# A tuned three-layer kernel: narrowing of the last layer's weights split in two parts, with a four-buffer target and a later cast

## The chip, the cores and the metric

The kernel runs on one core of a Trainium2 chip. The metric is the device time of one execution in microseconds. The kernel is timed in several runs; one more execution is profiled, and its trace is what the rows below come from. The engines are TensorE (PE, and PEld for its weight loads), VectorE (DVE), ScalarE (ACT), GpSimd (POOL) and SyncE (SP, which issues the transfers). Each takes its instructions strictly in the order of its own queue.

## The reference

Three layers follow each other. An attention with a running state gives 3072 tokens of 384 numbers. A mixture of 8 experts takes each token through one of them (384 to 1024 to 384, with a relu). The last layer is a gated unit whose weights come in 64-bit numbers:

```python
def _moe2_ref(x, w_gate, w_val, w_out):
    gate = 1.0 / (1.0 + np.exp(-(x @ w_gate)))    # w_gate, w_val: 384 x 1536
    val = x @ w_val
    return (gate * val @ w_out).astype(np.float32) # w_out: 1536 x 384
```

## The kernel before

All products run as three passes of a faster matmul type: each operand is split into a high part `h` (a cast on ScalarE) and a low part `l` (the operand minus its high part, on GpSimd or VectorE), and h x h, h x l, l x h are summed.

**The expert stage** (class `Experts`, about 350 to 615 us) works through 36 quarters: nine jobs (token windows) of four. A quarter holds two *places* (`f`), and a place is: nine matmuls `h` (L1151), a relu on ScalarE to `hh` (L1154), its low part `hl` on VectorE (L1155), and then the nine matmuls of the place before into `y` (L1114), of which three need `hl`. The expert weights `w1r` and `w2r` are loaded by SP and split with a cast `w1h`/`w2h` on ScalarE (L1087) and a subtraction `w1l`/`w2l` (L1092), most of them on GpSimd, some on VectorE. Rows of tokens `XR` are loaded from the table `disp`, scaled, and turned into `xh`/`xl`. The instructions that `Queue` issues (line L87) keep the written order; the others are ordered by the framework's scheduler, which takes what its own model of time finds ready. So the program's text sets an order of priority, and buffers and dependences decide what can be taken ahead.

**The last layer's weights** `w_gate` and `w_val` are brought in beside the experts, in 24 blocks of 384 x 128, by `hook`, which is called once in each place; from the 9th quarter on it deals with one block per quarter. Each block is

- loaded by SP as pairs of 32-bit words (`load_wide`, L987) into a tile of the ring XG, which has four buffers;
- narrowed from 64-bit to 32-bit numbers on VectorE by five operations (`narrow`, L998 to L1002): the first two take sign, exponent and upper bits from the high word into the result, the third and fourth make the rest from the low word, in the raw tile, and the fifth adds it. The result goes to the tile `xt`, of which there is one buffer;
- split by `split_hi_lo`: a cast to `wgh` or `wvh` on ScalarE (L974) and a subtraction to `wgl` or `wvl` on GpSimd (L975).

The last layer itself (L1465 on, from 615 us) narrows the 12 blocks of `w_out` with the same `narrow`, into the same `xt`, while its first token block runs.

Of the kernel before, what the change touches and what calls it, by code (L numbers as in the profile page):

```python
# [7 lines left out]
F32 = mybir.dt.float32  # L8
# [3 lines left out]
U32 = mybir.dt.uint32  # L12
AF = mybir.ActivationFunctionType
ALU = mybir.AluOpType
# [15 lines left out]
ROW = 386  # L30
# [941 lines left out]
def split_hi_lo(nc, hi, lo, src, eng, act=None):  # L972

    (act or nc.scalar).copy(out=hi, in_=src)  # L974
    eng.tensor_tensor(out=lo, in0=src, in1=hi, op=ALU.subtract)  # L975


def load_wide(queue, r, src, shape):

    wide = src.dtype != F32  # L980
    r = r[:, 0 : shape[0] * shape[1] * (2 if wide else 1)]
    if not wide:
        r = r.rearrange("p (a b) -> p a b", a=shape[0])
        queue.dma_start(out=r, in_=src)
        return r
    r = r.bitcast(U32)
    queue.dma_start(out=r.rearrange("p (a b) -> p a b", a=shape[0]), in_=src.bitcast(U32))  # L987
    return r.rearrange("p (a b t) -> p a b t", a=shape[0], t=2)


def narrow(nc, t, r):

    if r.dtype == F32:
        return r
    V = nc.vector
    u = t.bitcast(U32)
    lo, hi = r[..., 0], r[..., 1]
    V.tensor_scalar(out=u, in0=hi, scalar1=3, scalar2=0x3FFFFFFF, op0=ALU.logical_shift_left, op1=ALU.bitwise_and)  # L998
    V.scalar_tensor_tensor(out=u, in0=hi, scalar=0xC0000000, in1=u, op0=ALU.bitwise_and, op1=ALU.bitwise_or)
    V.tensor_scalar(out=hi, in0=u, scalar1=0xFF800000, scalar2=None, op0=ALU.bitwise_and)  # L1000
    V.scalar_tensor_tensor(out=lo.bitcast(F32), in0=lo, scalar=2.0**-52, in1=hi.bitcast(F32), op0=ALU.mult, op1=ALU.mult)
    V.tensor_tensor(out=t, in0=lo.bitcast(F32), in1=t, op=ALU.add)  # L1002
    return t


class Job:
# [161 lines left out]
def kernel_body(tc, a, out):  # L1168
    nc = tc.nc
    V, A, G, T, SP = nc.vector, nc.scalar, nc.gpsimd, nc.tensor, nc.sync  # L1170
    with ExitStack() as ctx:
# [10 lines left out]
        if True:  # L1182
# [13 lines left out]
            gs = ctx.enter_context(tc.tile_pool(name="gt_s", bufs=1, side="left"))  # L1196
# [42 lines left out]
            gv = [[yp.tile([128, 3, DF2], F32R, name=n + p) for p in "hl"] for n in ("wg", "wv")]  # L1239
# [40 lines left out]
            def gv_src(i):  # L1280
                b, w = divmod(i, 2)
                return w, slice(128 * b, 128 * b + 128), a[("m2g", "m2v")[w]].rearrange("(c p) f -> p c f", p=128)[:, :, 128 * b : 128 * b + 128]

            wide = {}
# [4 lines left out]
            queued, head = [], []  # L1289

            def first_high():

                for c in range(3):
                    A.copy(out=head[c], in_=y2T[:, c, 0:512])

            def hook(q, f):
                i = 2 * q + f
                if i == 0:
                    E.high(2)
                    E.low(2, 0, E.G)  # L1300
                    tail(1)
                elif i == 1:
                    tail(2)
                    tail(3)
                    E.low(2, 1, E.V)
                elif i == 2:
                    E.high(3)
                    E.low(3, 0, E.V)
                    E.low(3, 1, E.V)
                    E.n_split = 4  # L1310
                elif i == 3:
                    order()
                    E.rows(1)
                    E.load(6)
                if i == QX:
                    E.x_scale(1, (E.V, E.A))
                if i == QT:
                    for c in range(3):
                        E.x_turn(1, c)
                if i in (10, 12):  # L1320
                    E.split(E.n_split + 1)
                if i == 14:
                    queued.append(E.SP)
                    nc_ = tc.nc
                    E.use((nc_.vector, nc_.scalar, nc_.gpsimd, nc_.tensor, nc_.sync))
                if i == 10:
                    E.rows(2)
                if i == QS:
                    E.x_scale(2, (E.V,))
                if i == 13:  # L1330
                    for c in range(3):
                        E.x_turn(2, c)
                if i == SG:
                    A.activation(out=key[:, 0:1], in_=cst[0:1, 0:1], func=AF.Sigmoid)
                if i == YS:
                    head.extend(gs.tile([128, 2, ROW], F32, tag="XG", name="XG", bufs=4).rearrange("p a b -> p (a b)")[:, 0:512].bitcast(F32R) for _ in range(3))
                    first_high()
                if f == 0 or q < 8:
                    return
                q -= 8  # L1340
                if q < 24:
                    r = gs.tile([128, 2, ROW], F32, tag="XG", name="XG", bufs=4).rearrange("p a b -> p (a b)")
                    wide[q] = load_wide(queued[0] if q < 4 else SP, r, gv_src(q)[2], [3, 128])
                if 1 <= q < 25:
                    w, cols, _ = gv_src(q - 1)
                    f = narrow(nc, gs.tile([128, 3, 128], F32, tag="xt", name="xt", bufs=1), wide.pop(q - 1))
                    split_hi_lo(nc, *[t[:, :, cols] for t in gv[w]], f, G)

            with tc.tile_pool(name="ex_p", bufs=1, reuse_waits="tile", space=PSUM) as pp:
                E.run(y2T, pp, gp, hook, True)  # L1350
# [4 lines left out]
            with tc.If(placed < NTOK):  # L1355
                with tc.tile_pool(name="ov", bufs=1) as ov:
                    q = ov.tile([1, 2, 64 + NE * NW_], F32, name="ov_q")
# [47 lines left out]
            with ExitStack() as m2:  # L1405
# [8 lines left out]
                def wo_load(f):  # L1414
                    r = wide[:, 768 * (f % 2) : 768 * (f % 2) + 768]
                    r = load_wide(SP, r, a["m2o"][128 * f : 128 * f + 128].rearrange("p (o d) -> p o d", o=3), [3, 128])
                    r = narrow(nc, gs.tile([128, 3, 128], F32, tag="xt", name="xt", bufs=1), r)
                    split_hi_lo(nc, *[t[:, f].rearrange("p (o d) -> p o d", o=3) for t in wo], r, G)
# [13 lines left out]
                wide = sp.tile([128, 3, 512], F32R, tag="yh", name="yh", bufs=2).bitcast(F32).rearrange("p c t -> p (c t)")  # L1432
# [21 lines left out]
                for tb in range(6):  # L1454
                    Yn = None
                    ops_ = [pp.tile([128, 512], F32, tag=f"o{m}", name=f"o{m}") for m in range(4)]
                    for f in range(12):
# [17 lines left out]
                        if len(pend) == (4 if tb == 5 and f > 8 else 1):  # L1475
                            p = pend.pop(0)
# [75 lines left out]
```

## Time and profile before

| | before |
|---|---|
| median of 3 runs (all) | 1078.68 us (1072.25 to 1078.94) |
| the profiled execution: time, span | 1077.86 us, 1076.2 us |
| TensorE busy | 1016.2 us (94%) |
| VectorE busy | 547.4 us (51%) |
| ScalarE busy | 397.2 us (37%) |
| GpSimd busy | 313.5 us (29%) |

A matmul's end is modelled, so a busy TensorE is not one at its peak; where it is shown idle it did wait. "Held" below means that an operation took longer than its usual time. Times of a stretch are counted from the span's start.

### The profile page before, as it was taken

Reading aid. Unit: us, or ns where it says so; the run is one execution under the profiler, and the core shown is the slowest. Engines: PE = TensorE matmul, PEld = TensorE weight load, DVE = VectorE, ACT = ScalarE, POOL = GpSimd, SP = SyncE. Lnnn points to the kernel's source line nnn. Section 1 sums busy time; section 2 is a strip of 40 time slices with the busy share of each in tenths; the row PEclk is TensorE's granted clock in tenths of the full one; section 3 lists DMA queues with packets and bytes.
Section 4 is the critical chain, followed back from the end, with each engine's and each line's share of the span. In section 5 each row is a group of like instructions: output and inputs, shape, how many; then the busy total and the mean of one; then the engine's idle time right before and its main releaser. Section 6 shows DMA issues by size and latency. Waiting matters only on the chain. (4 is left out here: it accounts for less than half of the span.)

```text
span 1076.2 us, 22516 instructions
## 1 busy us (share of the span) xinstructions
PE 1016.2 (94%) x9111; PEld 919.6 (85%) x9112; DVE 547.4 (51%) x1498; ACT 397.2 (37%) x880; POOL 313.5 (29%) x304
## 2 busy tenths in 40 slices
PE   9778899997999999999889999999999999999997
PEld 8678888887889988788889988888888888888886
DVE  6968899999534577666683374511211211211211
ACT  6634545464443454454445322221212222212111
POOL 8520002102011234445443234332322311321322
PEclk9887577655565999999999999999999999999999
DMA  7999978654574365555544122000000000000000
GB/s 193 204 182 245 150 162 160 156 93 103 105 158 127 112 214 155 159 152 178 163 126 129 22 85 74 23 23 1 23 8 1 30 1 1 30 1 1 30 1 30
DMA packets 178366, 102.47 MB, mean 95 GB/s; under 512 B 126841, under 2 KB 166722, under 8 KB 178258
## 3 DMA queue, kind: packets, MB, share of 16 engines
q1 hardware_dynamic: 175186, 91.53, 35.8%
q0 software_dynamic: 3072, 9.46, 2.4%
q8 instruction: 73, 1.20, 0.5%
q14 instruction: 35, 0.29, 0.1%
HBM read 74.94 MB, written 15.80 MB: 84 GB/s over the span
## 5 line engine op out<-in xcount | busy, mean ns | idle before, releaser
L1473 DVE TENSOR_TENSOR gf<-gf,g 128x512 f32<-128x512 f32 x72 | 49.5, 688 | 308.9 <-PE g L1465 308.3
L975 POOL TENSOR_TENSOR gsl<-gf,gsh 128x512 fp32r<-128x512 f32 x68 | 88.5, 1302 | 270.1 <-ACT gsh L974 270.1
L1472 ACT ACTIVATE gf<-g 128x512 f32<-128x512 f32 x72 | 43.0, 598 | 184.5 <-PE g L1465 184.0
L974 ACT CAST gsh<-gf 128x512 fp32r<-128x512 f32 x69 | 42.8, 620 | 145.7 <-DVE gf L1473 145.1
L1439 PE MATMUL o<-woh,gsl 128*128 128x384 f32 x272 | 87.2, 338 | 0.0
L1439 PE MATMUL o<-wol,gsh 128*128 128x384 f32 x272 | 86.5, 337 | 0.0
L87 DVE TENSOR_TENSOR X<-X,tmp 128x84 f32<-128x84 f32 (+37 forms) x303 | 74.2, 275 | 0.8
L87 DVE TENSOR_TENSOR tmp<-X,Lt 128x84 f32<-128x84 f32 (+37 forms) x303 | 73.9, 274 | 1.4
L1155 DVE SCALAR_TENSOR_TENSOR hl<-h,hh 128x460 fp32r<-128x460 f32 (+7 forms) x57 | 33.1, 581 | 62.7 <-ACT hh L1154 62.6
L1114 PE MATMUL y<-hh,w2h 128*128 128x460 f32 (+6 forms) x168 | 60.9, 362 | 2.2 <-ACT hh L1154 2.1
L1465 PE MATMUL g<-yl,wgh 128*128 128x512 f32 x216 | 62.6, 395 | 0.0
L1465 PE MATMUL g<-yl,wvh 128*128 128x512 f32 x216 | 62.3, 395 | 0.0
L87 POOL COPY XG<-g_sc 128x2 f32<-128x2 f32 x24 | 6.0, 248 | 192.9 <-DVE g_sc L87 152.5
L1439 PE MATMUL o<-woh,gsh 128*128 128x384 f32 x272 | 61.7, 337 | 0.0
L1465 PE MATMUL g<-yh,wgh 128*128 128x512 f32 x180 | 60.9, 395 | 0.0
L87 PE MATMUL U<-W,TBD 64*64 64x48 f32 x768 | 42.0, 282 | 18.2 <-DVE W L87 11.3
L87 ACT ACTIVATE ks<-kth,rnt 128x48 f32<-128x48 f32 x192 | 54.5, 371 | 11.3 <-DMA kth<-in_ktok_dram 11.3
L1114 PE MATMUL y<-hh,w2l 128*128 128x460 f32 (+6 forms) x168 | 58.6, 349 | 0.0
L87 PEld LDWEIGHTS U<-W,TBD 64*64 64x64 f32 x768 | 38.3, 197 | 21.0 <-DVE W L87 12.6
L87 PE MATMUL GP<-KT,KB 112*64 112x64 f32 x640 | 47.7, 314 | 8.8 <-DMA KB<-in_st_dram 7.6
L1439 PEld LDWEIGHTS o<-woh,gsh 128*128 128x128 f32 x272 | 49.7, 188 | 5.8
L87 PEld LDWEIGHTS GP<-KT,KB 112*64 112x64 f32 x640 | 42.6, 221 | 13.2 <-POOL KH L87 6.5
(335 smaller groups left out, 2406.5 us busy)
## 6 DMA issues: line engine op xcount, KB each, us to landing
w1r<-in_w_dram SPq DMA_DIRECT2D x32, 384.0 KB
w2r<-in_w_dram SPq DMA_DIRECT2D x32, 384.0 KB
KT<-in_st_dram SPq DMA_DIRECT2D x20, 448.0 KB
disp<-TBD SPq DMA_DIRECT2D x8, 772.0 KB
kth<-in_ktok_dram SPq DMA_DIRECT2D x12, 384.0 KB
VT<-in_vtok_dram SPq DMA_DIRECT2D x12, 384.0 KB
KBD<-KH SPq DMA_DIRECT2D x48, 96.0 KB
XG<-in_m2g_dram SPq DMA_DIRECT2D x12, 384.0 KB
```

What stands on the lines that cost most here:

```text
L87: r = f(*args, **kw)
L974: (act or nc.scalar).copy(out=hi, in_=src)
L975: eng.tensor_tensor(out=lo, in0=src, in1=hi, op=ALU.subtract)
L1114: self.T.matmul(out=ys[c][:, 0:n], lhsT=w2[l][:, f % 2, 128 * c : 128 * c + 128], rhs=(hh, hl)[r], start=(f == 0 and i == 0), stop=(f == 7 ...
L1155: self.V.scalar_tensor_tensor(out=hl, in0=hp[:, 0:n], scalar=0.0, in1=hh, op0=ALU.max, op1=ALU.subtract)
L1439: T.matmul(out=ops_[m][:, 0:384], lhsT=gh[l][:, 128 * m : 128 * m + 128], rhs=wo[r][:, f], start=(f == 0 and i == 0), stop=(f == 11 and i ...
L1465: T.matmul(out=ps, lhsT=gv[w][l][:, c, 128 * f : 128 * f + 128], rhs=Y[r][c], start=(i == 0 and c == 0), stop=(i == 2 and c == 2))
L1472: A.activation(out=gf, in_=gps[0], func=AF.Sigmoid)
L1473: V.tensor_tensor(out=gf, in0=gf, in1=gps[1], op=ALU.mult)
```

## The change

`narrow` is cut in two: `narrow_top` (the first two operations) and `narrow_rest` (the other three). In `hook`, a block's load and its `narrow_top` now stand in the first place of a quarter (`f == 0`; they stood in the second), its `narrow_rest` in the second place of the same quarter as the top, and its `split_hi_lo` in the first place of the next quarter. The narrowed result goes to a tile of the XG ring instead of `xt`. A block so takes two of the ring's four buffers, one for the raw words and one for the result. The last layer's `narrow` calls both parts one behind the other, into `xt` as before. Lines behind `narrow` move by 15 (L1155 is L1170, L1092 is L1107), and L1000 to L1002 are now L1009 to L1011.

```diff
@@ -988,19 +988,34 @@
     return r.rearrange("p (a b t) -> p a b t", a=shape[0], t=2)


-def narrow(nc, t, r):
+def narrow_top(nc, t, r):
+
+    if r.dtype == F32:
+        return
+    V = nc.vector
+    u = t.bitcast(U32)
+    hi = r[..., 1]
+    V.tensor_scalar(out=u, in0=hi, scalar1=3, scalar2=0x3FFFFFFF, op0=ALU.logical_shift_left, op1=ALU.bitwise_and)
+    V.scalar_tensor_tensor(out=u, in0=hi, scalar=0xC0000000, in1=u, op0=ALU.bitwise_and, op1=ALU.bitwise_or)
+
+
+def narrow_rest(nc, t, r):

     if r.dtype == F32:
         return r
     V = nc.vector
     u = t.bitcast(U32)
     lo, hi = r[..., 0], r[..., 1]
-    V.tensor_scalar(out=u, in0=hi, scalar1=3, scalar2=0x3FFFFFFF, op0=ALU.logical_shift_left, op1=ALU.bitwise_and)
-    V.scalar_tensor_tensor(out=u, in0=hi, scalar=0xC0000000, in1=u, op0=ALU.bitwise_and, op1=ALU.bitwise_or)
     V.tensor_scalar(out=hi, in0=u, scalar1=0xFF800000, scalar2=None, op0=ALU.bitwise_and)
     V.scalar_tensor_tensor(out=lo.bitcast(F32), in0=lo, scalar=2.0**-52, in1=hi.bitcast(F32), op0=ALU.mult, op1=ALU.mult)
     V.tensor_tensor(out=t, in0=lo.bitcast(F32), in1=t, op=ALU.add)
     return t
+
+
+def narrow(nc, t, r):
+
+    narrow_top(nc, t, r)
+    return narrow_rest(nc, t, r)


 class Job:
@@ -1335,16 +1350,24 @@
                 if i == YS:
                     head.extend(gs.tile([128, 2, ROW], F32, tag="XG", name="XG", bufs=4).rearrange("p a b -> p (a b)")[:, 0:512].bitcast(F32R) for _ in range(3))
                     first_high()
-                if f == 0 or q < 8:
+                q -= 8
+                if q < 0:
                     return
-                q -= 8
+                place = lambda: gs.tile([128, 2, ROW], F32, tag="XG", name="XG", bufs=4).rearrange("p a b -> p (a b)")
+                if f:
+
+                    if q - 1 in wide:
+                        wide[q - 1] = narrow_rest(nc, *wide[q - 1])
+                    return
+                if q - 2 in wide:
+                    w, cols, _ = gv_src(q - 2)
+                    split_hi_lo(nc, *[t[:, :, cols] for t in gv[w]], wide.pop(q - 2), G)
+                if q - 1 in wide:
+                    t = place()[:, 0:384].rearrange("p (c f) -> p c f", c=3)
+                    narrow_top(nc, t, wide[q - 1])
+                    wide[q - 1] = t, wide[q - 1]
                 if q < 24:
-                    r = gs.tile([128, 2, ROW], F32, tag="XG", name="XG", bufs=4).rearrange("p a b -> p (a b)")
-                    wide[q] = load_wide(queued[0] if q < 4 else SP, r, gv_src(q)[2], [3, 128])
-                if 1 <= q < 25:
-                    w, cols, _ = gv_src(q - 1)
-                    f = narrow(nc, gs.tile([128, 3, 128], F32, tag="xt", name="xt", bufs=1), wide.pop(q - 1))
-                    split_hi_lo(nc, *[t[:, :, cols] for t in gv[w]], f, G)
+                    wide[q] = load_wide(queued[0] if q < 4 else SP, place(), gv_src(q)[2], [3, 128])

             with tc.tile_pool(name="ex_p", bufs=1, reuse_waits="tile", space=PSUM) as pp:
                 E.run(y2T, pp, gp, hook, True)
```

What the scheduler makes of it, on three pieces. First VectorE, in the places of the third job (460 tokens). `XG_n` with a number is a raw block or, as the target of L998, a narrowed one. Before:

```order
L998 TENSOR_SCALAR xt_7625<-XG_7551 128x384
L999 SCALAR_TENSOR_TENSOR xt_7625<-XG_7551,xt_7625 128x384
L1000 TENSOR_SCALAR XG_7551<-xt_7625 128x384
L1001 SCALAR_TENSOR_TENSOR XG_7551<-XG_7551 128x384
L1002 TENSOR_TENSOR xt_7625<-XG_7551,xt_7625 128x384
L1155 SCALAR_TENSOR_TENSOR hl_7334<-h_7323,hh_7333 128x460
L1092 TENSOR_TENSOR w2l_7341<-w2r_7252,w2h_7340 128x768
L998 TENSOR_SCALAR xt_7693<-XG_7623 128x384
L999 SCALAR_TENSOR_TENSOR xt_7693<-XG_7623,xt_7693 128x384
L1155 SCALAR_TENSOR_TENSOR hl_7365<-h_7354,hh_7364 128x460
```

The same two places now, behind the `hl` of the same place:

```order
L1009 TENSOR_SCALAR XG_7671<-XG_7761 128x384
L1010 SCALAR_TENSOR_TENSOR XG_7671<-XG_7671 128x384
L1011 TENSOR_TENSOR XG_7761<-XG_7671,XG_7761 128x384
L998 TENSOR_SCALAR XG_7842<-XG_7764 128x384
L999 SCALAR_TENSOR_TENSOR XG_7842<-XG_7764,XG_7842 128x384
L1170 SCALAR_TENSOR_TENSOR hl_7332<-h_7321,hh_7331 128x460
L1009 TENSOR_SCALAR XG_7764<-XG_7842 128x384
L1010 SCALAR_TENSOR_TENSOR XG_7764<-XG_7764 128x384
L1011 TENSOR_TENSOR XG_7842<-XG_7764,XG_7842 128x384
L1107 TENSOR_TENSOR w2l_7339<-w2r_7252,w2h_7338 128x768
L998 TENSOR_SCALAR XG_7914<-XG_7845 128x384
L999 SCALAR_TENSOR_TENSOR XG_7914<-XG_7845,XG_7914 128x384
```

Between the `hl` before these rows and the next but one stood five narrowing operations and then two; now there are five and five, of three blocks, and the tops of a block stand ahead of an `hl` and the rest behind it.

Second VectorE near the end of the fourth window (416 tokens), up to the 24th `hl` counted behind block 0. Before, it is block 13 that is narrowed there:

```order
L1155 SCALAR_TENSOR_TENSOR hl_7962<-h_7951,hh_7961 128x416
L998 TENSOR_SCALAR xt_8321<-XG_8251 128x384
L999 SCALAR_TENSOR_TENSOR xt_8321<-XG_8251,xt_8321 128x384
L1000 TENSOR_SCALAR XG_8251<-xt_8321 128x384
L1001 SCALAR_TENSOR_TENSOR XG_8251<-XG_8251 128x384
L1092 TENSOR_TENSOR w2l_7969<-w2r_7880,w2h_7968 128x768
L1002 TENSOR_TENSOR xt_8321<-XG_8251,xt_8321 128x384
L1155 SCALAR_TENSOR_TENSOR hl_7993<-h_7982,hh_7992 128x416
```

Now:

```order
L1011 TENSOR_TENSOR XG_9018<-XG_8928,XG_9018 128x384
L998 TENSOR_SCALAR XG_9099<-XG_9021 128x384
L999 SCALAR_TENSOR_TENSOR XG_9099<-XG_9021,XG_9099 128x384
L1009 TENSOR_SCALAR XG_9021<-XG_9099 128x384
L1010 SCALAR_TENSOR_TENSOR XG_9021<-XG_9021 128x384
L1170 SCALAR_TENSOR_TENSOR hl_7960<-h_7949,hh_7959 128x416
L1011 TENSOR_TENSOR XG_9099<-XG_9021,XG_9099 128x384
L1107 TENSOR_TENSOR w2l_7967<-w2r_7878,w2h_7966 128x768
L1170 SCALAR_TENSOR_TENSOR hl_7998<-h_7987,hh_7997 128x416
L1293 TENSOR_LOAD tab_6586
L1075 TENSOR_TENSOR xl_7876<-h_8031,xh_7875 128x404
L1170 SCALAR_TENSOR_TENSOR hl_8053<-h_8042,hh_8052 128x416
```

The block that ends here is the last one, 23; behind it VectorE has no narrowing left until the last layer, where before ten blocks followed.

Third SP, the loads in the third job (`XG` a block of the last layer's weights, `w1r` and `w2r` an expert's; ISA rows only prepare a transfer). Before:

```order
L1075 ISA
L1075 DMA w1r<-in_w_dram 128x3x256
L987 DMA XG<-in_m2v_dram 128x3x256
L1076 ISA
L1076 DMA w2r<-in_w_dram 128x2x384
L1075 ISA
L1075 DMA w1r<-in_w_dram 128x3x256
L987 DMA XG<-in_m2g_dram 128x3x256
L1076 ISA
L1076 DMA w2r<-in_w_dram 128x2x384
```

Now:

```order
L1090 ISA
L1090 DMA w1r<-in_w_dram 128x3x256
L987 DMA XG<-in_m2g_dram 128x3x256
L987 DMA XG<-in_m2v_dram 128x3x256
L1091 ISA
L1091 DMA w2r<-in_w_dram 128x2x384
L1090 ISA
L1090 DMA w1r<-in_w_dram 128x3x256
L987 DMA XG<-in_m2g_dram 128x3x256
L987 DMA XG<-in_m2v_dram 128x3x256
L1091 ISA
L1091 DMA w2r<-in_w_dram 128x2x384
```

Two block loads stand between the expert loads where one stood.

## Rows read from the trace of the kernel before

**Rows 1.** Windows, three stretches: length, busy PE, PEld, DVE, ACT, POOL; PEclk, DMA, GB/s

```profile
388.10:485.40 97.30, 93.23 (x495) 83.97 (x496) 70.24 (x113) 47.25 (x89) 40.60 (x27) 0.98 0.49 151
485.40:563.20 77.80, 70.17 (x389) 66.05 (x388) 57.27 (x87) 36.00 (x69) 36.07 (x23) 1.00 0.52 153
563.20:615.30 52.10, 50.75 (x293) 48.59 (x292) 16.64 (x28) 23.71 (x44) 17.65 (x10) 1.00 0.29 84
```

**Rows 2.** Groups by line, DVE, 388.1 to 485.4: busy us, mean ns, idle before

```profile
L999 DVE SCALAR_TENSOR_TENSOR xt<-XG,xt 128x384 uint32<-128x384 uint32 x13 | 11.0, 843 | 0.3
L1001 DVE SCALAR_TENSOR_TENSOR XG<-XG 128x384 f32<-128x384 uint32 x13 | 8.9, 685 | 0.3
L998 DVE TENSOR_SCALAR xt<-XG 128x384 uint32<-128x384 uint32 x13 | 7.9, 609 | 4.4 <-POOL wvl L975 3.4 <-POOL wgl L975 0.9
L1002 DVE TENSOR_TENSOR xt<-XG,xt 128x384 f32<-128x384 f32 x13 | 7.8, 596 | 0.4 <-DVE XG L1001 0.2
L1000 DVE TENSOR_SCALAR XG<-xt 128x384 uint32<-128x384 uint32 x13 | 7.4, 568 | 0.3
```

**Rows 3.** Groups by line, POOL, 388.1 to 485.4

```profile
L1092 POOL TENSOR_TENSOR w1l<-w1r,w1h 128x768 fp32r<-128x768 f32 x8 | 15.9, 1993 | 17.3 <-ACT w1h L1087 17.2
L1092 POOL TENSOR_TENSOR w2l<-w2r,w2h 128x768 fp32r<-128x768 f32 x6 | 11.3, 1889 | 15.2 <-ACT w2h L1087 13.1 <-PE h L1151 2.1
L975 POOL TENSOR_TENSOR wgl<-xt,wgh 128x384 fp32r<-128x384 f32 x7 | 7.8, 1120 | 16.2 <-ACT wgh L974 16.2
L975 POOL TENSOR_TENSOR wvl<-xt,wvh 128x384 fp32r<-128x384 f32 x6 | 6.9, 1148 | 8.8 <-ACT hh L1154 4.6 <-ACT wvh L974 4.2
```

**Rows 4.** Tile `xt`, whole span: duration ns min/median/max, first and last start us

```profile
L998 DVE TENSOR_SCALAR xt<-XG x24: 348/360/2032, 382.0 to 557.5; 128x384 uint32<-128x384 uint32 x24
L999 DVE SCALAR_TENSOR_TENSOR xt<-XG,xt x24: 545/559/2115, 382.6 to 557.9; 128x384 uint32<-128x384 uint32 x24
L1000 DVE TENSOR_SCALAR XG<-xt x24: 345/361/1996, 383.2 to 560.1; 128x384 uint32<-128x384 uint32 x24
L1002 DVE TENSOR_TENSOR xt<-XG,xt x24: 541/558/2092, 385.7 to 562.1; 128x384 f32<-128x384 f32 x24
```

**Rows 5.** Timeline of DVE around 450 us: start us, us, instruction

```profile
449.37 1.97 DVE L1000 TENSOR_SCALAR XG<-xt 128x384 uint32<-128x384 uint32 x1
451.37 0.56 DVE L1001 SCALAR_TENSOR_TENSOR XG<-XG 128x384 f32<-128x384 uint32 x1
451.96 0.56 DVE L1002 TENSOR_TENSOR xt<-XG,xt 128x384 f32<-128x384 f32 x1
452.44 0.60 DVE L1155 SCALAR_TENSOR_TENSOR hl<-h,hh 128x436 fp32r<-128x436 f32 x1
```

**Rows 6.** Timeline of POOL, the same moment; in brackets idle before and releaser

```profile
449.28 1.84 POOL L1092 TENSOR_TENSOR w1l<-w1r,w1h 128x768 fp32r<-128x768 f32 x1 [0.37 <-ACT w1h L1087]
```

**Rows 7.** Timeline of PE, the same moment

```profile
453.10 0.85 PE L1151 MATMUL h<-xh,w1h 128*128 128x436 f32 x3 [1.91 <-DVE hl L1155]
```

**Rows 8.** Timeline of POOL in the last layer

```profile
625.61 2.66 POOL L975 TENSOR_TENSOR gsl<-gf,gsh 128x512 fp32r<-128x512 f32 x2
```

**Rows 9.** Timeline of DVE at the same moment

```profile
625.66 1.46 DVE L998 TENSOR_SCALAR xt<-yh 128x384 uint32<-128x384 uint32 x1
```

**Rows 10.** Waits of PE, 485.4 to 563.2: us in total, times, longest

```profile
PE h L1151 <- DVE hl L1155: 2.9, 1, 2.9
PE y L1114 <- ACT hh L1154: 2.1, 2, 1.2
PE nm L1127 <- DMA XR<-disp: 1.6, 2, 1.3
PE h L1151 <- DVE xl L1060: 0.8, 1, 0.8
```

**Rows 11.** Waits of DVE, 388.1 to 485.4, the longest of them

```profile
DVE hl L1155 <- ACT hh L1154: 18.5, 12, 3.9
```

**Rows 12.** Tile XG, 360 to 620 us, its transfers

```profile
DMA to landing us min/median/max: 2.7/3.0/3.4
```

## Prediction

> **What bounds the kernel now.** I read the windows view first, cut at four moments: 388.1 us, where block 0 of the last layer's weights has been narrowed; 485.4 us, the end of the 24th `hl` from there (`hl` is VectorE's low half of the hidden layer, one for each place, that is each half of a quarter of an expert); 563.2 us, just behind the last narrowing of the expert stage; 615.3 us, the first matmul of the last layer. I call the three stretches A, B and C. The reader is to see that TensorE is nearly full in all three: 93.23 of 97.30 us, 70.17 of 77.80 and 50.75 of 52.10 [rows 1]. So TensorE is the bound, and all that its waiting costs here is 4.1 + 7.6 + 1.4 = 13 us, about 1.2% of the kernel. No better placing of the narrowing can give more. VectorE is second: 70.24 us of 97.30 in A, so 27.1 us idle; 57.27 of 77.80 in B; 16.64 of 52.10 in C [rows 1].
>
> Then I asked what VectorE's time in A is made of. The five operations of `narrow` take 11.0 + 8.9 + 7.9 + 7.8 + 7.4 = 43.0 us for 13 blocks [rows 2]; everything else (24 `hl`, the `xl`, the low parts of expert weights, the copies of results) takes 70.24 - 43.0 = 27.2 us. The medians of the five are 0.36, 0.56, 0.36, 0.56 and 0.56 us [rows 4, 5], 2.40 us a block, so 13 blocks should take 31.2 us. The other 11.8 us are waiting inside the operations, and the timeline shows for what: L1000 starts at 449.37, takes 1.97 us instead of 0.36, and ends just after GpSimd's low part of an expert weight, which ran from 449.28 for 1.84 us [rows 5, 6]. `hl` stands behind it on VectorE and starts at 452.44; TensorE waits 1.91 us for it [rows 5, 7]. So TensorE's stalls come from narrowing that GpSimd holds up, ahead of an `hl`.
>
> **What the change removes, adds and moves.** No arithmetic is added: five VectorE operations, a ScalarE cast, a GpSimd subtraction and one load for each of 24 blocks, as before. Two things change. The cast stands later, so that ScalarE's `hh` does not wait for a narrowing right ahead of it. And the narrowed block goes to the XG ring (4 buffers) instead of the single `xt`. The second matters most. Before, a block's first operation overwrites `xt` and must wait for GpSimd's subtraction of the block before; the scheduler therefore spread the 24 blocks up to the last `hl` of 396 columns. Without that wait it hoists them: the first piece of VectorE's order shows ten narrowing operations in two places (from one `hl` to the next) where seven stood, and the second shows the last block, 23, finished just ahead of the `hl` that ends A. (Counted along both orders: between the `hl` that bound A stand 13 blocks before and 23 after, 65 and 115 operations.) The queues are strictly in order, so this packing is forced on the chip too.
>
> *VectorE in A.* Narrowing 23 x 2.40 = 55.2 us, the rest 27.2 us unchanged: 82.4 us without any holding. TensorE's own work in A is 93.2 us [rows 1]. The margin is 10.8 us, less than the 11.8 us of holding that are there already with 13 blocks.
>
> *Holding in A.* The 14 expert low parts on GpSimd take 15.9 + 11.3 = 27.2 us, 1.94 each, and the 13 subtractions of narrowed blocks 7.8 + 6.9 = 14.7 us, 1.13 each [rows 3]. Before, the latter can't hold anything up, since the next narrowing waits for them on `xt`; now nothing prevents it. That L975 does hold a narrowing operation is seen in the last layer, where the same line subtracts something else at that moment: GpSimd's `gsl` from 625.61 (two of 1.33 us) makes L998 take 1.46 us [rows 8, 9]. Bounds: nothing new, 11.8 us; everything held for its full length, 27.2 + 23 x 1.13 = 53.2 us. In between: VectorE will be narrowing in 55.2/82.4 = 67% of its unheld time, so two in three GpSimd operations meet a narrowing, which then waits for their length less half an operation (0.24 us): 14 x 0.67 x 1.70 = 15.9 and 23 x 0.67 x 0.89 = 13.7, together 29.6 us. The same formula for before (31.2/58.4 = 53%, the 14 alone) gives 12.6 us against 11.8 measured, so I take it.
>
> The Trainium skill ("SBUF — State Buffer", "SBUF: two separate sides") says that VectorE and GpSimd share a port pair under an exclusive lock: who starts first holds it for the whole instruction and the other is fully blocked. The held rows above agree. By that rule every one of the 23 subtractions is a holder as the expert parts are, the sum below; if only the expert parts held, as in stretch A before, 13.7 us would fall out and the time would be about 1078 us.
>
> *Idle time of VectorE in A.* Of 27.1 us before, 18.5 are `hl` waiting for `hh` [rows 11], that is for TensorE. With VectorE behind, these go; what stays is the few light places and a load that comes late. Bounds 0 and 15 us, I take 5.
>
> So A takes 82.4 + 29.6 + 5 = 117 us instead of 97.3: **+19.7 us**.
>
> *B.* It has no narrowing left (10 blocks before). TensorE's waits there for `hl`, `hh` and `xl`, 2.9 + 2.1 + 0.8 = 5.8 us, go; the 1.6 us for rows of `disp` stay [rows 10]: **-5.8 us**. C has neither now: 0.
>
> *Cover of the parts I cost at nothing.* The loads: a raw block now has two buffers instead of four, so its load is issued only after the last narrowing step of the block two before, and lands 3.0 us later (2.7 to 3.4) [rows 12]. Meanwhile VectorE does the block between, 2.40 us, an `hl`, 0.6, and some 1.2 of holding: 4.2 us, enough by about 1 us. If the cover is gone, 22 loads late by 1 us are +22 us. Behind a waiting load on SP's queue stand the expert weights (the piece of SP's order); counted along the orders, each is wanted two or more places later, so they have a place to spare. GpSimd: 40.6 us of 97.3 busy [rows 1], plus 10 subtractions, 11 us: 52 of 117. ScalarE gets ten short casts more in A and was busy 47.25 of 97.30 us [rows 1].
>
> **Sum.** The profiled execution has a span of 1076.2 us and a time of 1077.86, 0.8 below the median of the runs, 1078.68. 1077.9 + 19.7 - 5.8 = 1091.8. I say 1092 us.
>
> **Rivals.** 1: *VectorE keeps up* (the other side, not slower). The decisive thing is holding plus idle in A: at 82.4 + 20.7 us A takes 97.3 + 5.8, and the kernel is even. With 11.8 us of holding and 2 of idle A would take 96.2 us, and the time is 1077.9 - 1.1 - 5.8 = 1071. For it: GpSimd's subtraction may mostly fall under an `hl`, as it does in A before. Against it: VectorE would be filled to 97% while TensorE still needs each `hl` in time. 2: *Late loads.* Two raw buffers don't cover 3.0 us, VectorE waits for XG at the head of its queue, `hl` behind it: +22 us, partly in place of the holding, some 1105 to 1115. For it: loads come about twice as dense in A beside the expert weights; against it: holding itself gives them time. 3: *The split does nothing*: TensorE's slack of a place at each side absorbs the denser narrowing, A grows by what B saves. That needs holding plus idle near 20 us; 1076 to 1083.
>
> **How the numbers follow.** Chances: mine 0.50 (1083 to 1105), rival 1 0.13, rival 2 0.12, rival 3 0.25. What a measurement can tell from no change is about 1%, here under 1068 or over 1089.5. Mine lies over that bound in four fifths of its cases, 0.40, with rival 2 0.52 slower; rival 1 gives 0.05 under 1068; the rest, 0.43, is the same. Range: holding of 18 to 45 us and idle of 2 to 10 give A 102 to 137, so 1077 to 1112; I take 1075 to 1110.
>
> **What would show it.** VectorE busy for over 90% from 388 us to the 24th `hl` after it, and that `hl` ending near 505 instead of 485.4; narrowing operations held by `wgl` and `wvl` on L975, their total in the expert stage near 80 us or more; TensorE waiting for `hl` in most places of A, and hardly at all after block 23; `hh` no longer behind a cast that waits. Wrong in the holding, if the five operations stay at their present mean; wrong in the loads, if the first operation of a block waits for XG; wrong altogether, if that `hl` ends before 491.

## The result, and the profile after

The changed kernel takes 1086.87 us (median of 19 runs, 1078.83 to 1093.79), the kernel before beside it 1077.72 us. The ratio is 1.0086, 95% interval 1.0063 to 1.0108: slower by 9.3 us, with 6.8 to 11.6 us from the interval. That is inside the forecast range of 1075 to 1110, on the forecast side, and a little under the 1% that the text took as the bound of "slower". Two of the twelve runs of experiment e9 below, 1079.69 and 1082.71 us, fell in a slower state and are left out of its ratio (the medians of all its runs would give 0.996).

The profiled execution has a span of 1080.0 us, 3.8 more than before. That difference understates the change, because the stages ahead of the experts differ from one execution to the next: the first narrowing begins at 382.0 us before, at 374.5 after, and at 390.1 in experiment e1, whose program is that of before. So I compare the expert stage alone, from the end of the `hl` of the place where block 0 is begun in these two kernels (the same `hl` in every experiment) to the first matmul of the last layer. It takes 232.6 us before and 244.0 after, +11.4; what follows it takes 460.9 and 460.8.

The windows of the changed kernel, cut at the same four events as [rows 1] (columns as there):

```profile
380.60:499.00 118.40, 100.10 (x495) 88.54 (x496) 108.13 (x163) 51.89 (x99) 51.40 (x37) 0.93 0.50 154
499.00:566.10 67.10, 66.81 (x380) 64.36 (x379) 22.36 (x36) 32.28 (x58) 24.07 (x14) 1.00 0.47 134
566.10:619.20 53.10, 51.89 (x303) 50.17 (x301) 16.77 (x28) 23.77 (x43) 16.64 (x9) 1.00 0.30 85
```

Stretch A grew from 97.3 to 118.4 us (+21.1; forecast 117), B shrank from 77.8 to 67.1 (-10.7; forecast -5.8), C went from 52.1 to 53.1. In A VectorE is busy 108.13 of 118.40 us, 91% instead of 72%. TensorE makes the same 495 matmuls and is shown idle for 18.3 us instead of 4.1.

VectorE's groups in A, where [rows 2] has 13 of each (L1009 to L1011 were L1000 to L1002); columns are busy us, mean ns, idle before and its releaser:

```profile
L1010 DVE SCALAR_TENSOR_TENSOR XG<-XG 128x384 f32<-128x384 uint32 x23 | 19.3, 839 | 0.4
L999 DVE SCALAR_TENSOR_TENSOR XG<-XG 128x384 uint32<-128x384 uint32 x23 | 18.7, 812 | 0.4
L1011 DVE TENSOR_TENSOR XG<-XG 128x384 f32<-128x384 f32 x23 | 17.0, 738 | 0.3
L1009 DVE TENSOR_SCALAR XG<-XG 128x384 uint32<-128x384 uint32 x23 | 16.8, 733 | 0.3
L998 DVE TENSOR_SCALAR XG<-XG 128x384 uint32<-128x384 uint32 x23 | 14.2, 618 | 8.0 <-DMA XG<-in_m2g_dram 6.2 <-DMA XG<-in_m2v_dram 1.7
```

23 blocks take 86.0 us; unheld they would take 55.2. So 30.8 us are holding; the forecast had 29.6.

What VectorE waited for in A ([rows 11] has one line of it from before; us in total, times, longest):

```profile
DVE XG L998 <- DMA XG<-in_m2g_dram: 6.2, 3, 3.1
DVE XG L998 <- DMA XG<-in_m2v_dram: 1.7, 3, 0.8
DVE hl L1170 <- ACT hh L1169: 0.4, 1, 0.4
```

`hl` waited 18.5 us for `hh` before and waits 0.4 now: VectorE is behind, and TensorE waits for it. What remains of its idle time is late loads. TensorE's waits in A:

```profile
PE y L1129 <- DVE hl L1170: 6.4, 5, 2.1
PE y L1129 <- ACT hh L1169: 4.6, 4, 2.9
PE nm L1142 <- DMA XR<-disp: 4.0, 1, 4.0
PE h L1166 <- DVE hl L1170: 2.1, 1, 2.1
PE nm L1142 <- ACT XR L1144: 1.1, 1, 1.1
PE h L87 <- DVE hl L87: 0.7, 1, 0.7
```

The 4.0 us for rows of `disp` go back to VectorE too, at least in part. That load was issued at 470.52 us, next on SP's queue behind a load of `w2r` that SP issued only at 469.44, just after a `w2l` on VectorE had ended at 469.41. SP's own wait there, which the profile puts down to the VectorE operation beside that `w2l`:

```profile
SPq L1091 <- DVE XG L1009: 4.6, 1, 4.6
```

A piece of the timeline shows both ways in which VectorE falls behind, VectorE first and then GpSimd:

```profile
429.31 1.07 DVE L1009 TENSOR_SCALAR XG<-XG 128x384 uint32<-128x384 uint32 x1
430.29 0.60 DVE L1170 SCALAR_TENSOR_TENSOR hl<-h,hh 128x436 fp32r<-128x436 f32 x1
435.97 1.54 DVE L998 TENSOR_SCALAR XG<-XG 128x384 uint32<-128x384 uint32 x1 [3.06 <-DMA XG<-in_m2g_dram]
```

```profile
429.03 1.12 POOL L975 TENSOR_TENSOR wgl<-XG,wgh 128x384 fp32r<-128x384 f32 x1 [2.38 <-ACT wgh L974]
```

L1009 takes 1.07 us instead of 0.36 because GpSimd subtracts a narrowed block from 429.03 to 430.15, and `hl` stands behind it. Before, such a subtraction never met a narrowing: in A their records overlap by 0.0 us. Then, up to 435.97 us, the head of the queue waits 3.06 us for a block that has not landed.

### The profile page after: what moved, and what is told of

It reads as the page before. It is cut to its first block, busy times and chain, and to the rows that moved or that the text cites. A ratio compares the mean times of both kernels' runs of the same rounds, so it can differ in the third digit from the quotient of the medians.

```text
span 1080.0 us, 22520 instructions
## 1 busy us (share of the span) xinstructions
PE 1012.6 (94%) x9111; PEld 916.2 (85%) x9112; DVE 552.2 (51%) x1498; ACT 398.1 (37%) x880; POOL 314.8 (29%) x304
## 5 line engine op out<-in xcount | busy, mean ns | idle before, releaser
L1170 DVE SCALAR_TENSOR_TENSOR hl<-h,hh 128x460 fp32r<-128x460 f32 (+7 forms) x57 | 33.0, 580 | 68.0 <-ACT hh L1169 67.7
L1462 PEld LDWEIGHTS o<-wol,gsh 128*128 128x128 f32 x272 | 50.7, 188 | 2.4
```

The lines of the kernel that those rows point to most:

```text
L1170: self.V.scalar_tensor_tensor(out=hl, in0=hp[:, 0:n], scalar=0.0, in1=hh, op0=ALU.max, op1=ALU.subtract)
L1462: T.matmul(out=ops_[m][:, 0:384], lhsT=gh[l][:, 128 * m : 128 * m + 128], rhs=wo[r][:, f], start=(f == 0 and i == 0), stop=(f == 11 and i ...
```

## The experiments

Times of single runs spread by about 1%, so ratios are to the kernel before on the same chip. "Stage" is the expert stage in the profiled execution, as above, and "holding" is the time of all narrowing operations of its 24 blocks less 24 x 2.40 us.

| kernel | ratio, 95% interval | stage us | holding us | places with narrowing |
|---|---|---|---|---|
| before | 1 | 232.6 | 28.5 | 45 |
| after | 1.0086 (1.0063 to 1.0108) | 244.0 | 33.8 | 26 |
| e1: split, into `xt` | 1.0016 (0.9991 to 1.0041) | 231.6 | 28.5 | 45 |
| e2: whole, into the ring | 1.0070 (1.0042 to 1.0098) | 241.1 | 31.8 | 27 |
| e3: after without subtractions | 1.0000 (0.9971 to 1.0028) | 230.5 | 19.6 | 26 |
| e4: after, tied to its places | 0.9947 (0.9921 to 0.9973) | 228.4 | 39.8 | 49 |
| e5: before, tied | 0.9994 (0.9960 to 1.0029) | 232.8 | 36.3 | 48 |
| e7: e4, into `xt` | 0.9969 (0.9943 to 0.9995) | 229.7 | 41.8 | 49 |
| e8: e4, twice as dense | 1.0083 (1.0048 to 1.0118) | 244.7 | 36.3 | 28 |
| e9: e4, cast at once | 0.9949 (0.9914 to 0.9984) | 227.6 | 39.8 | 49 |

The last column counts, along VectorE's order, the places from the first narrowing operation to the last.

**e1: is it the split or the target?** In the changed kernel:

```diff
-                    t = place()[:, 0:384].rearrange("p (c f) -> p c f", c=3)
+                    t = gs.tile([128, 3, 128], F32, tag="xt", name="xt", bufs=1)
                     narrow_top(nc, t, wide[q - 1])
```

> The change without the ring as target: narrowing in two places and the cast a third place later, but into the single xt. Theory (the four-buffer target is what packs the narrowing, and the packing costs): the scheduler gives the order of before, 65 narrowing operations in stretch A, so the time of before, ratio 1.000 within 0.004, stretch A near 97 us. Rival (the split itself or the later cast costs): 1083 to 1088 us.

The built program has the instructions of the kernel before in the same order on every engine, line numbers apart: the scheduler hoists both parts as it hoisted the whole, and only the single `xt` holds it back. So this run is also a null test. Its stretch A as a window, and two of its narrowing groups there:

```profile
396.20:492.50 96.30, 91.65 (x495) 82.62 (x496) 70.07 (x114) 47.47 (x89) 40.46 (x27) 1.00 0.51 153
```

```profile
L999 DVE SCALAR_TENSOR_TENSOR xt<-XG,xt 128x384 uint32<-128x384 uint32 x13 | 11.0, 845 | 0.3
L1010 DVE SCALAR_TENSOR_TENSOR XG<-XG 128x384 f32<-128x384 uint32 x13 | 8.9, 684 | 0.3
```

These repeat [rows 2] to 0.1 us, holding and all. Splitting the narrowing and moving the cast did nothing by themselves.

**e2: the target alone.** In the kernel before:

```diff
-                    f = narrow(nc, gs.tile([128, 3, 128], F32, tag="xt", name="xt", bufs=1), wide.pop(q - 1))
+                    t = gs.tile([128, 2, ROW], F32, tag="XG", name="XG", bufs=4).rearrange("p a b -> p (a b)")
+                    f = narrow(nc, t[:, 0:384].rearrange("p (c f) -> p c f", c=3), wide.pop(q - 1))
```

> The kernel before with one edit: the narrowed block goes into the ring XG instead of xt; narrowing whole, cast right behind it. Theory (packing): 113 of the 115 narrowing operations stand in stretch A as in the change, so it costs what the change costs, 1084 to 1093 us, ratio 1.006 to 1.014, stretch A 115 to 122 us. Rival (split and later cast cost): the time of before, 1074 to 1081.

Its window of A:

```profile
385.20:499.10 113.90, 98.24 (x498) 85.54 (x498) 110.52 (x163) 51.29 (x98) 52.71 (x37) 0.97 0.53 157
```

One edit gives a loss that can't be told from that of the change, with VectorE 97% busy in A. A is a little under what was expected (113.9 against 115 to 122): here no wait of VectorE for a load is listed, where the changed kernel waits 7.9 us. So the loss does not need the late loads. Why they are missing here is not shown.

**e3: do the subtractions of narrowed blocks hold VectorE?** The changed kernel without GpSimd's subtractions of the 24 blocks; a second cast on ScalarE writes the low half, which so holds the block itself:

```diff
-                    split_hi_lo(nc, *[t[:, :, cols] for t in gv[w]], wide.pop(q - 2), G)
+                    src = wide.pop(q - 2)
+                    for t in gv[w]:
+                        A.copy(out=t[:, :, cols], in_=src)
```

> The changed kernel, but the low halves of the 24 blocks are made by a second cast on ScalarE instead of the subtraction on GpSimd (so they hold the block itself, not its low part). Theory (subtractions of narrowed blocks hold VectorE for about 13.7 of 30.8 us in stretch A): holding in A 15 to 19 us, A 103 to 107 us instead of 118, time 1072 to 1077 us. Rival a (only the expert weights' subtractions hold, as before): holding stays near 30, time 1083 to 1088. Rival b (late loads bound A): A stays above 112 because the waits for XG grow as the holding falls.

Its window of A and the narrowing groups in it:

```profile
390.60:495.80 105.20, 94.45 (x495) 84.10 (x496) 93.76 (x163) 60.92 (x123) 25.26 (x13) 0.98 0.57 173
```

```profile
L1011 DVE TENSOR_TENSOR XG<-XG 128x384 f32<-128x384 f32 x23 | 17.3, 753 | 0.2
L999 DVE SCALAR_TENSOR_TENSOR XG<-XG 128x384 uint32<-128x384 uint32 x23 | 14.3, 623 | 0.3
L1010 DVE SCALAR_TENSOR_TENSOR XG<-XG 128x384 f32<-128x384 uint32 x23 | 14.3, 622 | 0.5
L998 DVE TENSOR_SCALAR XG<-XG 128x384 uint32<-128x384 uint32 x23 | 13.2, 574 | 8.4 <-DMA XG<-in_m2g_dram 7.2 <-DMA XG<-in_m2v_dram 1.3
L1009 DVE TENSOR_SCALAR XG<-XG 128x384 uint32<-128x384 uint32 x23 | 12.7, 552 | 0.4
```

The five now take 71.8 us, so holding is 16.6 instead of 30.8: 14.2 us went with the subtractions (forecast 13.7), and A falls from 118.4 to 105.2. The waits for loads stay at 8.4 us, so they did not take the place of the holding. With the same dense order the loss against before is gone (1.0000). What is left in A over 97.3 is paid by B, which has no narrowing in this kernel either.

**e4: the order tied to the written places.** In the changed kernel, `self.hl` being the instruction that makes `hl`:

```diff
+                        with tc.issue_after(E.hl):
                             wide[q - 1] = narrow_rest(nc, *wide[q - 1])
...
+                    with tc.issue_after(E.hl):
                         narrow_top(nc, t, wide[q - 1])
```

> The changed kernel with its narrowing tied behind the hl of the place in which it is written, so that 2 and 3 narrowing operations stand in alternate places up to the end of the expert stage (60 in stretch A instead of 115). Theory (density of narrowing against hl decides): TensorE's waits for hl and hh, 5.8 us in stretch B and some 3 in A of the kernel before, nearly go; expert stage 222 to 227 us instead of 233 before and 245 after; time 1066 to 1072 us, ratio to before 0.990 to 0.995. Rival (what counts is that a narrowing is held at all, at any density): hl is late as often as before, 1075 to 1081.

The window from the first narrowing to the last, TensorE's waits in the expert stage, and the narrowing groups:

```profile
406.50:592.40 185.90, 180.54 (x979) 166.17 (x978) 144.65 (x212) 92.10 (x170) 87.99 (x56) 1.00 0.57 167
```

```profile
PE h L1166 <- DVE xl L1075: 2.6, 5, 0.7
...
PE h L1166 <- DVE hl L1170: 0.8, 2, 0.6
PE y L1129 <- ACT hh L1169: 0.8, 2, 0.4
```

```profile
L1010 DVE SCALAR_TENSOR_TENSOR XG<-XG 128x384 f32<-128x384 uint32 x24 | 28.9, 1202 | 0.6
L999 DVE SCALAR_TENSOR_TENSOR XG<-XG 128x384 uint32<-128x384 uint32 x24 | 24.7, 1028 | 0.3
L1009 DVE TENSOR_SCALAR XG<-XG 128x384 uint32<-128x384 uint32 x24 | 20.9, 872 | 0.0
L1011 DVE TENSOR_TENSOR XG<-XG 128x384 f32<-128x384 f32 x24 | 13.4, 557 | 0.7
L998 DVE TENSOR_SCALAR XG<-XG 128x384 uint32<-128x384 uint32 x24 | 9.6, 399 | 0.0
```

This kernel beats both, 0.9947. The stage, 228.4 us, is 1.4 over the expected span, the time within it. And it holds *more*: 39.8 us for 24 blocks, against 33.8 in the changed kernel. With two or three narrowing operations ahead of an `hl` and VectorE 78% busy, TensorE waits 1.6 us for `hl` and `hh` in the whole stage. So holding does no harm by itself here; with VectorE 91% busy it does (below).

**e8: dense, but even.** One block for every place, its five operations tied behind that place's `hl` (in `hook`, with `p` counting places):

```diff
...
+                if p - 2 in wide:
+                    t = place()[:, 0:384].rearrange("p (c f) -> p c f", c=3)
+                    with tc.issue_after(E.hl):
+                        wide[p - 2] = narrow(nc, t, wide[p - 2])
+                if p < 24:
+                    wide[p] = load_wide(queued[0] if p < 4 else SP, place(), gv_src(p)[2], [3, 128])
```

> Kernel e4 (tied behind the hl of its place, ring as target), but one block for every place instead of every second: five narrowing operations ahead of nearly every hl, all 24 blocks within 28 places. Theory (density of narrowing decides, however evenly it is dealt out): VectorE over 90% busy in the places that narrow, holding 28 to 40 us, expert stage 236 to 244 us, time 1081 to 1089 us. Rival (only the scheduler's uneven clumps of 7 to 9 operations hurt): TensorE hardly waits, stage 228 to 233 us, time 1071 to 1077 us.

Its window from the first narrowing to the last, and TensorE's largest waits in the expert stage:

```profile
406.20:537.40 131.20, 113.62 (x569) 101.68 (x568) 119.95 (x171) 57.67 (x106) 66.71 (x43) 0.96 0.56 164
```

```profile
PE h L1166 <- DVE hl L1170: 10.9, 5, 3.6
PE nm L1142 <- DMA XR<-disp: 3.3, 2, 2.2
```

VectorE is 91% busy, TensorE waits 11.3 us for `hl`, and the loss of the change is back (1.0083; the stage, 244.7 us, 0.7 over the expected span). So it is the density, and the scheduler's clumps are not needed for it. But density alone does not do it: e3 is as dense as the change, holds 19.6 us instead of 33.8, and comes out even. It is density together with the holding by the blocks' subtractions.

**e5, e7, e9: which of the tied kernel's parts matter.** e5 ties the whole narrowing of the kernel before in the same way:

```diff
-                    f = narrow(nc, gs.tile([128, 3, 128], F32, tag="xt", name="xt", bufs=1), wide.pop(q - 1))
+                    t = gs.tile([128, 3, 128], F32, tag="xt", name="xt", bufs=1)
+                    with tc.issue_after(E.hl):
+                        f = narrow(nc, t, wide.pop(q - 1))
```

e7 is e4 with the edit of e1, the target `xt`. e9 is e4 with `split_hi_lo` moved up behind `narrow_rest`:

```diff
                             wide[q - 1] = narrow_rest(nc, *wide[q - 1])
+                        split_hi_lo(nc, *[t[:, :, cols] for t in gv[w]], wide.pop(q - 1), G)
...
-                if q - 2 in wide:
-                    split_hi_lo(nc, *[t[:, :, cols] for t in gv[w]], wide.pop(q - 2), G)
```

> The kernel before (whole narrowing, cast at once, single xt), its narrowing tied behind the hl of the place in which it is written: five operations in every other place, up to the end of the expert stage. Theory (it is the number of narrowing operations ahead of one hl that makes it late): five in one place with one or two held are 4 to 6 us against a place of some 3.8, so hl is late in part of the places; TensorE waits for hl and hh 4 to 9 us in the expert stage, time 1073 to 1078 us, ratio 0.997 to 1.002. Rival (an even pace over the stage is enough, the split adds nothing): as e4, 1068 to 1073 us, ratio 0.992 to 0.996.

> Kernel e4 (split, later cast, tied to the written places) with the single xt as target instead of the ring. Theory (with the order tied, the target's buffers no longer decide anything, since GpSimd has long subtracted a block when the next one's first part is due): as e4, expert stage 226 to 231 us, ratio to before 0.992 to 0.998. Rival (the ring is needed, because the first part waits for GpSimd on xt at the head of VectorE's queue): VectorE waits for GpSimd at the first operation of a block, more than 8 us in total, ratio 0.999 or more.

> Kernel e4 with the cast and the subtraction right behind the second part of the narrowing instead of a third place later. Theory (the later cast matters little, for with 2 and 3 operations a place ScalarE's hh rarely stands behind a cast that waits): as e4 within 3 us, expert stage 227 to 232 us, ratio to before 0.992 to 0.998. Rival (hh stands behind the waiting cast in every second place): TensorE waits more than 4 us for hh, ratio 0.999 or more.

TensorE's waits in e5, then VectorE's waits for `xt` in e7, then TensorE's waits in e9, all in the expert stage:

```profile
PE h L1151 <- DVE xl L1060: 6.2, 5, 2.0
PE nm L1127 <- DMA XR<-disp: 4.1, 5, 1.7
PE y L1114 <- DVE hl L1155: 1.2, 2, 0.9
PE y L1114 <- ACT hh L1154: 1.0, 1, 1.0
```

```profile
DVE xt L998 <- POOL wvl L975: 3.9, 4, 1.2
...
DVE xt L998 <- POOL wgl L975: 1.7, 3, 1.2
```

```profile
PE h L1166 <- DVE hl L1170: 0.8, 2, 0.6
PE y L1129 <- ACT hh L1169: 0.7, 1, 0.7
```

e5 is no faster than before, as the theory had it, but by another wait than I expected: 2.2 us for `hl` and `hh` (4 to 9 expected), and 6.2 us for `xl`, which in these five waits stands behind three or four operations of one block. Its interval overlaps that of e4 a little (0.9960 to 0.9973), so that the split pays under a tied order is likely, with 4.4 us of stage between the two profiles, but not beyond doubt. In e7 VectorE waits 5.6 us for GpSimd on `xt` (none was expected, over 8 by the rival), and TensorE 6.2 us for `hl`, against 0.8 in e4. So the target still decides something; but e7's ratio, between e4 and before, can't be told apart from that of e4. e9 can't be told from e4 (0.9949 and 0.9947): the cast's third place has no effect that these runs can see.

What was not tried: a ring of five or six buffers, which might take the late loads away; what these cost by themselves in the changed kernel is not shown.

## Why the prediction was right, point by point

*The cause was right.* It said that not the split but the target packs the narrowing into A and makes VectorE the bound there. e1 and e2 separate the two: the split and the later cast alone give the program of before, the ring alone gives the loss.

*A, 117 us forecast, 118.4 measured.* The holding formula gave 29.6 us and the trace 30.8; its two parts, 15.9 for the expert weights' subtractions and 13.7 for those of the blocks, were 16.6 and 14.2 by e3. Two terms beside it were off and cancelled, which is luck. VectorE's other work was put at 27.2 us, the window's busy time less the groups' sum; the same difference is now 108.13 - 86.0 = 22.1 us. The instructions are the same (48 of them take 31.6 us one by one before and 30.6 after); but records of neighbours overlap, and a window counts an overlap once where the groups' sum counts it twice. In the denser order more falls away: 8.5 us of A instead of 4.3. The idle time was put at 5 us and was 10.3, of which 7.9 are late loads: rival 2 came true for a third of its price, beside the holding and not in its place.

*The landing of a load.* The 3.0 us that the prediction took from [rows 12] is not that of a block's load. The view takes in every transfer that names a tile XG, and the only two with a landing in the kernel before are GpSimd's writes to `disp`. In the list of issues from 350 us on (four of those writes), where the last figure is the median time to landing if there is one, before and then after:

```profile
XG<-in_m2g_dram SPq DMA_DIRECT2D x12, 384.0 KB
disp<-XG,g_pos POOLq DMA_INDIRECT x4, 2.8
```

```profile
XG<-in_m2g_dram SPq DMA_DIRECT2D x12, 384.0 KB, 4.1
```

In the changed kernel six of the 24 loads have a landing on record, 3.2 to 5.0 us after the issue, median 3.9. So the cover of 4.2 us was not "enough by about 1 us", which fits the 7.9 us of late loads. How long a block's load took in the kernel before, these views do not show.

*The lock.* The forecast took every subtraction of a narrowed block for a holder; without that it would have been 1078 us. e3 is that case made real, 1.0000 of before with 14.2 us less holding. In the trace of the changed kernel itself, if each lengthened operation is put down to the GpSimd instruction that it overlaps most, 18.5 us fall to the expert weights and 13.0 to the blocks. The Trainium skill ("SBUF — State Buffer", "SBUF: two separate sides") says that of a GpSimd operation and a VectorE operation that uses the shared ports, whichever starts first has them for its whole instruction, and the other fully blocks. The trace agrees, for subtractions of about 1.1 us as for those of 1.9.

*B and C, -5.8 us forecast, -9.7 measured.* The waits for `hl`, `hh` and `xl` are gone, and so is most of the 1.6 us for rows of `disp`, which I had left standing: B is shown idle for 0.3 us instead of 7.6. That makes 7.5 us with C. The other 2.2 us are in TensorE's busy time (118.7 instead of 120.9 us in B and C together, for 683 matmuls instead of 682). Since a matmul's end is modelled, waits shorter than its tail may count as busy; whether that is all, no run settles.

*The sum.* +13.9 us forecast, +11.4 in the profiles' expert stages, +9.3 by the ratio of the runs. The direction, the mechanism and the range held. The 1092 us was 5 high: about half of that is B and C, less what A lacked, and the rest is the difference between two single profiles and the medians.

*What I got wrong beside the sum.* "ScalarE's `hh` does not wait for a narrowing right ahead of it" did not come true. ScalarE's casts of A:

```profile
ACT wgh L974 <- DVE XG L1011: 31.6, 11, 5.7
ACT wvh L974 <- DVE XG L1011: 20.0, 10, 3.8
```

They wait 51.6 us for the last narrowing step, 21.9 before, and TensorE waits 4.6 us in A for `hh`, each of the four times for one that stands behind such a cast. The cast is later in the program, but in VectorE's backlog the narrowing is later still. And TensorE did not wait for `hl` in most places of A but in seven, 9.2 us in total; the rest of its loss in A is waits for `hh` and rows of `disp`, and a lower clock (below). The other signs came: that `hl` ends at 499.0 and not near 505 only because the stage began 7.5 us sooner, and the 24 blocks take 91.4 us, where 80 or more was named.

*Rivals.* That VectorE keeps up needed holding plus idle under 20.7 us in A; it was 41.1. Rival 3, that the kernel comes out even, is what e3 shows when the subtractions go.

## What to carry to other kernels

A single buffer can be what paces work that a scheduler is free to hoist. Before giving such a tile more buffers, count along the built order how many of its operations then stand between two results that the bounding engine waits for, add what the neighbour engine holds up, and compare with the time the bounding engine gives per result. Here five operations per place were too many when both kinds of subtraction held them (e8, 1.0083), came out even without the blocks' subtractions (e3, 1.0000), and two or three per place gained although they were held most of all (e4, 0.9947). So spread the work over the whole stage, by a tie to the place where it is written, rather than let it run ahead.

## What the runs showed of the hardware that I had not expected

TensorE's clock fell in A of the changed kernel: the granted clock is 0.93 on average, against 0.98 before, with four drops to the lower level (1.2 GHz) of 3.4 to 6.8 us. The same 495 matmuls were busy for 100.1 us instead of 93.2. Ahead of each drop TensorE had been waiting: it was busy 7.62 of 11.30 us up to the first (416.3 us), and 3.62 of 5.20, 2.81 of 5.30 and 3.80 of 7.80 us up to the others (440.2, 457.3 and 477.8). I had priced none of it. As far as these rows go it did not add to the sum: VectorE's busy time and its listed waits make 116.4 of the 118.4 us, and of the waits only 0.4 us are for work behind TensorE, so TensorE was slower in time in which it would have waited. Nor does the loss need so many drops: e2 has it with a granted clock of 0.97 in A. Where TensorE is the bound a drop does cost, by these two profiles about 1 us: the kernel before has one in A (0.98, 97.3 us), and e1, the same program, has none (1.00, 96.3 us).

An operation that is held shows in the profile as a long operation (L1009 above, 1.07 us instead of 0.36) and not as idle time. Of such time 39.8 us were hidden in VectorE's slack in e4, where it is 78% busy, and 33.8 us were not in the changed kernel, where it is 91% busy.
